# Moving the closing arithmetic of finished head groups behind the next step's products on VectorE, in a one-core decode attention kernel

## The chip, the core and the metric

The kernel runs on one core of a Trainium2 chip. The metric is device time in microseconds (us) of one execution, from first to last instruction of the core with what lies around it. Smaller is better. Several engines of the core run side by side, each with a queue of its own that it works off in order: TensorE (PE in the profile, PEld its weight loads), VectorE (DVE), ScalarE (ACT), GpSimd (POOL) and SyncE (SP), which here issues nearly all DMA transfers. An engine that reaches an instruction whose input isn't there waits, and everything behind it in its queue waits with it.

## The reference, cut to what matters

One decode step (one new token, batch of 2) of a pre-norm transformer block: attention with 32 heads of 128 over a cache of 8192 positions, and a gated feed-forward part. All tensors are bf16.

```python
def _A_ref(x, k_cache, v_cache, wq, wo):          # x: [2, 1, 512], caches: [2, 32, 8192, 128]
    q = (x @ wq).reshape(B, Sq, Hq, Dh).transpose(0, 2, 1, 3)
    scores = jnp.einsum("bhqd,bhkd->bhqk", q, k_cache) * (Dh ** -0.5)
    p = _softmax(scores, axis=-1)
    o = jnp.einsum("bhqk,bhkd->bhqd", p, v_cache)
    return o.transpose(0, 2, 1, 3).reshape(B, Sq, Hq * Dh) @ wo

h  = x + _A_ref(_layernorm(x), A_k_cache, A_v_cache, A_wq, A_wo)
h2 = h + _B_ref(_layernorm(h), B_W_gate, B_W_up, B_W_down)   # ((relu(x Wg) * (x Wu)) Wd)
```

Nearly all of the data are the two caches: 2 x 2 x 32 x 8192 x 128 values of two bytes, 268 MB, each read once.

## The kernel before, in words

**Steps.** The cache is worked through in steps. Steps 0 to 14 take four heads of one batch row each (a "quad"; `Q = LASTQ = 14`), and two last half steps, `p0` and `p1`, take two heads each. A quad's K tile and V tile are 8.39 MB each, [128 partitions x 32768] bf16. Three such buffers exist (`bufs`). Step i has its K in buffer 2i mod 3 and its V in buffer 2i+1 mod 3, so V of step i+1 goes where K of step i was, and K of step i+2 where V of step i was.

**What a step does.** `scores_pe(s)` (L329 on) lets TensorE and ScalarE compute the scores of the last 24 to 32 of the tile's 256 slots of 128 values. `products(s)` (L374 to L378) lets VectorE multiply the remaining slots by the query, one instruction of up to 128 x 29696 values, and `scores(s)` (L388 to L402) adds the products up in four halvings (L396), a reduction (L398) and a maximum (L402). `largest_of_own(s)` (L411 to L420) finds the maximum per head and issues the exponentials on ScalarE, `place_own(s)` (L422 to L426) spreads them into the operand `pg`, and `values(s, u0, u1)` (L443 to L454) issues products u0 to u1 of 64 that multiply the exponentials with V on TensorE.

**Groups.** After steps 3, 7 and 11 four quads are complete, after step 14 three more. `diagonals(i)` (L456) then gathers the group's unnormalised output in PSUM (`o_ps`). What closes a group is the function `close(i)` (L318 to L322), four parts: `own_sums(i)` (L297 to L302, VectorE, prepares the sums of exponentials in `zc`), `sums(i)` (L304 to L308, a TensorE product with ones that gives the denominators in `z_ps`), `shares(i)` (L310 to L312, VectorE, the reciprocal `rz`) and `normalise(i)` (L314 to L316, VectorE, output times reciprocal into `ocol`). In the loop (L518 to L556) `close(i - 1)` stands in steps 4, 8 and 12, behind the step's first eight value products.

**W_o's first rows.** In step 12 the kernel also calls `spread(0, b)` (L479 to L488, two VectorE products that lay 16 finished heads out in `qrep`), and, after eight more value products, `lay_rows(0, ..., scalar=True)` (L490 to L497): two TensorE products into `or_ps` and one ScalarE copy into `orow`.

**What sets the order.** The schedule is written by hand (`manual_schedule`): each engine executes its instructions in the order of the program text. SyncE issues a load when its buffer is free: V of step i+1 behind `scores(i)`, K of step i+2 behind `values(i)`. All of these loads go through one queue, and the transfers follow each other in it, each split over the 16 DMA engines.

**The end.** After the loop come the last quad, `p0` and `p1`, the loads of W_o (`wo`), the gate, up and down weights (`wgu`, `wd_sb`), the output product, the second normalisation and the feed-forward part (L651 to L723). The last weights to arrive are those of `wd_sb`, needed by the products `d_ps` of L712.

Of the kernel before, what the change touches and what calls it, by code (L numbers as in the profile page):

```python
# [13 lines left out]
def _free(t, offset, dims):  # L14

    return bass.AP(tensor=t.tensor, offset=t.offset + offset, ap=[t.ap[0]] + [list(d) for d in dims])
# [7 lines left out]
def kernel(  # L24
# [15 lines left out]
    B, Sq, D = A_x.shape  # L40
# [117 lines left out]
    Q = LASTQ  # L158

    def load_tile(cache, s, dst, pieces=1):  # L160
        h = NH * s.g + (0 if s.quad else 2 * s.k)
        n = s.nt * Dh
        w = n // pieces
        for k in range(pieces):
            nc.sync.dma_start(
                out=dst[:, k * w:(k + 1) * w], in_=_dram(cache, (s.b * Hkv + h) * Sk * Dh + k * w, [[n, P], [1, w]]),
            )
# [19 lines left out]
    with tc.manual_schedule():  # L187
# [94 lines left out]
        def place_q(s):  # L282
            nc.scalar.activation(out=qz[:, QZ - NH:QZ], in_=qTs[:, s.b, NH * s.g:NH * (s.g + 1)], func=ACT.Copy)

        groups = {3: (0, 0, 4), 7: (0, 4, 4), 11: (1, 0, 4), 14: (1, 4, 3)}
# [4 lines left out]
        def heads(i):  # L290
            if i > Q:
                k = i - Q - 1
                return B - 1, Hq - NH + 2 * k, 2, zc[:, B - 1, NQ - 1, 2 * k:2 * k + 2]
            b, g0, n = groups[i]
            return b, NH * g0, NH * n + (2 if i == Q else 0), zc[:, b, g0:g0 + n, :]

        def own_sums(i):  # L297
            b, g0, n = groups[i]
            nc.vector.tensor_tensor(
                out=zc[:, b, g0:g0 + n, :], in0=_free(zs, b * NQ + g0, [[1, n], [0, NH]]),  # L300
                in1=_free(own, 0, [[0, n], [1, NH]]), op=ALU.mult,
            )  # L302

        def sums(i):  # L304

            _, _, n, z = heads(i)
            z_ps[i] = ps.tile([P, n], f32, tag="mx", name="z_ps")
            nc.tensor.matmul(out=z_ps[i], lhsT=ones, rhs=z, start=True, stop=True)  # L308

        def shares(i):  # L310
            rzs[i] = small.tile([P, heads(i)[2]], f32, tag="rz", name="rz", bufs=2)
            nc.vector.reciprocal(out=rzs[i], in_=z_ps[i])  # L312

        def normalise(i):  # L314
            b, h0, n, _ = heads(i)
            nc.vector.tensor_tensor(out=ocol[:, h0:h0 + n, b], in0=o_ps[i][:, 0:n], in1=rzs[i], op=ALU.mult)  # L316

        def close(i):  # L318
            own_sums(i)
            sums(i)  # L320
            shares(i)
            normalise(i)  # L322

        scols = {
            i: qrep[:, c0:c0 + n].rearrange("p i d -> p (i d)").bitcast(f32)
            for i, c0, n in ((Q, 6, 4), (Q + 1, 10, 2), (Q + 2, 12, 2))
# [47 lines left out]
        def products(s, t0=0, t1=None):  # L374

            n = (s.nv if t1 is None else t1) - t0
            kv = _free(s.kt, t0 * Dh, [[Dh, n], [1, Dh]])
            nc.vector.tensor_tensor(out=kv, in0=kv, in1=_free(s.qr, 0, [[0, n], [1, Dh]]), op=ALU.mult)  # L378
# [9 lines left out]
        def scores(s):  # L388

            scol = scols[s.i]  # L390
            width = Dh
            while width > 8:
                half = width // 2
                lo = _free(s.kt, s.na * Dh, [[Dh, s.nv - s.na], [1, half]])
                hi = _free(s.kt, s.na * Dh + half, [[Dh, s.nv - s.na], [1, half]])
                nc.vector.tensor_tensor(out=lo, in0=lo, in1=hi, op=ALU.add)  # L396
                width = half
            nc.vector.tensor_reduce(  # L398
                out=scol[:, s.na:s.nv], in_=_free(s.kt, s.na * Dh, [[Dh, s.nv - s.na], [1, 8]]), axis=AXIS.X, op=ALU.add,
            )  # L400
            pms[s.i] = small.tile([P, 1], f32, tag="pm", name="pm", bufs=2)
            nc.vector.tensor_reduce(out=pms[s.i], in_=scol, axis=AXIS.X, op=ALU.max)  # L402
# [8 lines left out]
        def largest_of_own(s):  # L411
            pm32 = small.tile([P, 32], f32, tag="pm32", name="pm32")
            nc.vector.transpose(out=pm32, in_=_free(pms[s.i], 0, [[0, 32]]))  # L413
            hmax = small.tile([P, 1], f32, tag="hmax", name="hmax")
            nc.vector.tensor_reduce(out=hmax, in_=pm32, axis=AXIS.X, op=ALU.max)  # L415
            nmax = small.tile([P, 1], f32, tag="nmax", name="nmax", bufs=2)
            nc.vector.tensor_scalar_mul(nmax, hmax, -SCALE)  # L417
            nc.scalar.activation(  # L418
                out=ecol, in_=scols[s.i], func=ACT.Exp, scale=SCALE, bias=nmax, accum_out=zs[:, s.b, s.g:s.g + 1],
            )  # L420

        def place_own(s):  # L422
            nc.vector.tensor_tensor(  # L423
                out=s.pg, in0=_free(ecol, 0, [[VG, s.nt // VG], [0, NH], [1, VG]]),
                in1=_free(ownb, 0, [[0, s.nt // VG], [VG, NH], [1, VG]]), op=ALU.mult,
            )  # L426
# [16 lines left out]
        def values(s, u0, u1):  # L443

            r = slice(32 * (s.g % 4), 32 * (s.g % 4) + s.nh * VG)
            if u0 == 0:
                pv_ps[s.i] = ps2.tile([P, VG * Dh], f32, tag="o", name="pv_ps")
            for u in range(u0, u1):
                nc.tensor.matmul(  # L449
                    out=pv_ps[s.i][r, :], lhsT=s.pg[:, u].rearrange("p j t -> p (j t)"),  # L450
                    rhs=s.vt[:, u * VG * Dh:(u + 1) * VG * Dh], start=(u == 0), stop=(u == s.nt // VG - 1),
                )
            if u1 == s.nt // VG:
                nc.scalar.activation(out=pv[r, :], in_=pv_ps[s.i][r, :], func=ACT.Copy)  # L454
# [24 lines left out]
        def spread(k, b):  # L479

            h0, n, _ = SETS[k]
            nq = Dh // n
            sp = qrep[:, B * k + b, :]
            nc.vector.tensor_tensor(
                out=_free(sp, 0, [[nq, n], [1, nq]]), in0=_free(ocol, h0 * B + b, [[B, n], [0, nq]]),
                in1=_free(quot[n], 0, [[0, n], [1, nq]]), op=ALU.mult,
            )
            return sp  # L488

        def lay_rows(k, sps, scalar=False):  # L490

            r = SROWS[k]
            or_ps = ps.tile([P, B, r], f32, tag="mx")
            for b in range(B):
                nc.tensor.matmul(out=or_ps[:, b, :], lhsT=sps[b], rhs=rest[r], start=True, stop=True)
            if scalar:
                nc.scalar.activation(out=orow[k], in_=or_ps.rearrange("p b c -> p c b"), func=ACT.Copy)  # L497
            else:
                nc.vector.tensor_copy(orow[k], or_ps.rearrange("p b c -> p c b"))
# [18 lines left out]
        for i in range(Q):  # L518
            s = steps[i]
            scols[i] = small.tile([P, s.nt], f32, tag="scol", name="scol")  # L520
            scores_pe(s)
            place_q(steps[i + 1])
            products(s)
            scores(s)
            if i == Q - 2:
                load_tile(A_k_cache, steps[Q], steps[Q].kt)
            else:
                load_tile(A_v_cache, steps[i + 1], steps[i + 1].vt)
            if i == Q - 1:
                scores_pe(steps[Q])  # L530
            largest_of_own(s)
            if i == Q - 1:
                products(steps[Q], 0, NEXT)
            place_own(s)
            half = s.nt // VG // 2
            ahead = 8 if i - 1 in groups else 0
            if ahead:
                values(s, 0, ahead)
                close(i - 1)
            if i == 12:  # L540
                sps = [spread(0, b) for b in range(B)]
                values(s, ahead, 2 * ahead)
                ahead *= 2
                lay_rows(0, sps, scalar=True)
            values(s, ahead, half)
            if i == Q - 1:
                load_tile(A_k_cache, steps[Q + 1], steps[Q + 1].kt)
            values(s, half, 2 * half)
            if i in groups:
                diagonals(i)  # L550
            if i + 2 < Q:
                load_tile(A_k_cache, steps[i + 2], steps[i + 2].kt)
            elif i == Q - 2:
                load_tile(A_v_cache, steps[Q - 1], steps[Q - 1].vt)
            else:
                load_tile(A_k_cache, steps[Q + 2], steps[Q + 2].kt)  # L556


        s, p0, p1 = steps[Q:]
# [76 lines left out]
        sps = [[spread(k, b) for b in range(B)] for k in range(1, len(SETS))]  # L636
# [117 lines left out]
```

## Time and profile before

| what | value |
|---|---|
| median of three runs | 661.1 us (660.15 to 661.72) |
| the profiled execution: time | 660.24 us |
| its span in the trace | 658.5 us (so 1.74 us lie around the span) |
| VectorE busy | 557.5 us, 85% of the span |
| TensorE busy | 349.5 us, 53% |
| ScalarE busy | 123.1 us, 19% |
| queue of the loads | 281.09 MB, 99.0% of 16 engines' span, 427 GB/s |
| VectorE waiting for K tiles (L378) | 36.9 us in 11 waits |
| VectorE waiting for `z_ps` ahead of the reciprocal (L312) | 12.6 us in 4 waits, the longest 4.1 us |

All times below are us from the start of the span unless marked ns. A row of the timeline names start, duration, engine, line, operation, output and inputs, and in square brackets how long the engine had been idle just before and what ended the idle time. A row of the DMA view gives the time from issue to the landing of the last byte. The chain of waits is the work that ended last, followed back from the last instruction, at each step to what released it.

### The profile page before, as it was taken

What the parts mean: (1) busy time and instruction counts of PE and PEld (TensorE: products, weight loads), DVE (VectorE), ACT (ScalarE), POOL (GpSimd) and SP (SyncE); (2) the same over time, 40 slices, a digit from 0 to 9 for tenths busy, and PEclk for the clock granted to TensorE, in tenths of its full rate; (3) what the DMA queues carried; (4) which work ended last, traced back from release to release, by engine and by line L of the source; (5) the groups of instructions that cost most, each with busy time, mean ns of one, the idle gap of its engine ahead of it and who ended that gap; (6) DMA issues with size and microseconds to landing.
All of it is one profiled execution on the core that took longest, in us unless ns stands there. A gap on an engine that the chain in (4) does not pass through costs nothing.

```text
span 658.5 us, 5118 instructions
## 1 busy us (share of the span) xinstructions
PE 349.5 (53%) x2123; PEld 159.0 (24%) x2123; DVE 557.5 (85%) x248; ACT 123.1 (19%) x335; POOL 7.0 (1%) x35
## 2 busy tenths in 40 slices
PE   2530924709175380926538092562909458191997
PEld 1220311304022130312214031221403224030456
DVE  2399697988979799897979979896997969999981
ACT  1130030300203030030302103030210304201870
POOL 3000000000000000000000000000000000000000
PEclk9875876958678595877959587695958869686895
DMA  9999999999999999999999999999999999999997
GB/s 382 446 443 446 402 431 438 446 446 396 442 438 439 434 427 430 438 430 435 438 426 443 426 438 431 430 439 442 422 430 431 438 443 426 430 429 425 424 417 278
DMA packets 7946, 281.40 MB, mean 427 GB/s; under 512 B 882, under 2 KB 1780, under 8 KB 2804
## 3 DMA queue, kind: packets, MB, share of 16 engines
q1 hardware_dynamic: 7920, 281.09, 99.0%
q8 instruction: 16, 0.26, 0.1%
q14 instruction: 6, 0.05, 0.0%
q10 hardware_dynamic: 4, 0.00, 0.0%
HBM read 281.09 MB, written 0.00 MB: 427 GB/s over the span
## 4 chain that ended last, share of the span: by engine, by line
DVE 52%; DMA 29%; PE 18%; issue 1%; ACT 1%; SPq 0%; DVEq 0%; ACTq 0%
DMA tile<-in_A_k_cache_dram 29%; DVE tile L378 23%; DVE tile L396 22%; PE pv_ps L449 15%; DVE scol L398 3%; DVE pgq L423 1%; ACT ecol L418 1%; DVE pm L402 1%; DVE qrep L398 1%; PE o_ps L472 1%; DVE pm L413 0%; PE z_ps L308 0%; PE att_ps L505 0%; PE d_ps L701 0%; DVE hmax L415 0%
## 5 line engine op out<-in xcount | busy, mean ns | idle before, releaser
L449 PE MATMUL pv_ps<-tile,pgq 128*16 128x512 bf16 x960 | 240.7, 416 | 240.8 <-DVE pgq L423 227.8
L378 DVE TENSOR_TENSOR tile<-tile,qrep 128x29696 bf16<-128x29696 bf16 (+3 forms) x16 | 232.4, 14522 | 36.9 <-DMA tile<-in_A_k_cache_dram 36.9
L396 DVE TENSOR_TENSOR tile<-tile 128x14848 bf16<-128x14848 bf16 (+7 forms) x68 | 236.5, 3477 | 2.3
L449 PEld LDWEIGHTS <-pgq 128*16 128x16 bf16 x960 | 90.6, 96 | 379.9 <-DVE pgq L423 239.7
L353 ACT ACTIVATE tile<-t_ps 128x1024 bf16<-128x1024 bf16 x53 | 52.6, 1022 | 16.6 <-PE t_ps L352 16.1
L454 ACT ACTIVATE pv<-pv_ps 16x512 f32<-16x512 f32 (+1 forms) x16 | 9.4, 590 | 232.5 <-PE pv_ps L449 232.5
L418 ACT ACTIVATE ecol<-scol,nmax 128x256 bf16<-128x256 f32 x14 | 7.1, 508 | 201.0 <-DVE nmax L417 201.0
L352 PE MATMUL t_ps<-ident,tile 128*128 128x128 bf16 x424 | 31.7, 226 | 16.5 <-DMA tile<-in_A_k_cache_dram 16.5
L343 PE MATMUL row_ps<-tile,qz 128*24 128x512 bf16 (+1 forms) x98 | 29.6, 383 | 18.9 <-ACT tile L353 18.9
L352 PEld LDWEIGHTS <-tile 128*128 128x128 bf16 x424 | 25.4, 102 | 31.4 <-DMA tile<-in_A_k_cache_dram 17.1
L398 DVE TENSOR_REDUCE scol<-tile 128x232 f32<-128x1856 bf16 (+1 forms) x14 | 28.9, 2068 | 0.5
L423 DVE TENSOR_TENSOR pgq<-ecol,ownb 128x1024 bf16<-128x1024 bf16 x15 | 10.4, 692 | 10.3 <-ACT ecol L418 10.3
L384 ACT ACTIVATE tile<-tile 128x128 bf16<-128x128 bf16 x60 | 17.6, 294 | 1.9 <-DVE tile L378 1.9
L378 DVE TENSOR_TENSOR tile<-tile,qpair 128x4096 bf16<-128x4096 bf16 (+3 forms) x4 | 15.5, 3884 | 0.0
L252 DVE CAST tile<-q_ps 2x512 bf16<-2x512 f32 x8 | 5.4, 679 | 10.9 <-PE q_ps L249 10.9
L343 PEld LDWEIGHTS <-qz 128*24 128x24 bf16 (+1 forms) x98 | 7.8, 92 | 28.3 <-issue 22.8
L249 PE MATMUL q_ps<-tile,xn 128*2 128x512 bf16 x32 | 10.2, 486 | 8.4 <-DMA tile<-in_A_wq_dram 8.4
L370 ACT ACTIVATE scol<-sc_ps 32x24 f32<-32x24 f32 (+1 forms) x56 | 11.7, 210 | 7.7 <-PE sc_ps L365 7.2
L365 PE MATMUL sc_ps<-ident_f,tile 24*128 24x24 f32 (+2 forms) x68 | 7.2, 221 | 11.0 <-ACT tile L361 11.0
L361 ACT ACTIVATE tile<-row_ps 24x512 f32<-24x512 f32 (+2 forms) x17 | 10.0, 586 | 13.5 <-PE row_ps L343 13.5
L312 DVE RECIPROCAL rz<-z_ps 128x16 f32<-128x16 f32 (+1 forms) x4 | 0.9, 236 | 12.6 <-PE z_ps L308 12.6
L384 ACT ACTIVATION_READ_ACCUMULATOR tile<-tile 128x1 f32 x60 | 11.2, 187 | 0.0
(130 smaller groups left out, 130.8 us busy)
## 6 DMA issues: line engine op xcount, KB each, us to landing
tile<-in_A_k_cache_dram SPq DMA_DIRECT2D x2, 4096.0 KB, 21.7
tile<-in_A_wq_dram SPq DMA_DIRECT2D x1, 4096.0 KB, 12.4
tile<-in_A_v_cache_dram SPq DMA_DIRECT2D x1, 4096.0 KB, 19.4
tile<-in_A_v_cache_dram SPq DMA_DIRECT2D x4, 1024.0 KB, 20.5
tile<-in_A_wo_dram SPq DMA_DIRECT2D x1, 2048.0 KB, 23.8
tile<-in_B_W_gate_dram SPq DMA_DIRECT2D x2, 688.0 KB, 13.6
tile<-in_B_W_up_dram SPq DMA_DIRECT2D x2, 688.0 KB, 12.4
tile<-in_A_wo_dram SPq DMA_DIRECT2D x1, 1024.0 KB
```

Of the source, the lines that this page charges most:

```text
L249: nc.tensor.matmul(out=q_ps, lhsT=xn[:, c, :], rhs=wq_sb[:, c, n0:n0 + 4 * Dh], start=(c == 0), stop=(c == KC - 1),)
L343: nc.tensor.matmul(out=row_ps, lhsT=z, rhs=s.kt[:, (nv + c0 + k) * Dh:(nv + c0 + k + 4) * Dh], start=(u == 0), stop=(u == U - 1),)
L352: nc.tensor.transpose(t_ps[:, k, :], s.kt[:, t * Dh:(t + 1) * Dh], ident)
L353: nc.scalar.activation(out=s.kt[:, (nv + c0) * Dh:(nv + c0 + TPC) * Dh], in_=t_ps.rearrange("p t s -> p (t s)"), func=ACT.Copy,)
L370: nc.scalar.activation(out=scols[s.i][r, nv:s.nt].rearrange("p (u t) -> p t u", t=4), in_=sc_ps[r, :, :, j], func=ACT.Copy,)
L378: nc.vector.tensor_tensor(out=kv, in0=kv, in1=_free(s.qr, 0, [[0, n], [1, Dh]]), op=ALU.mult)
L384: nc.scalar.activation(out=kv, in_=kv, func=ACT.Copy, accum_out=scols[s.i][:, t:t + 1])
L396: nc.vector.tensor_tensor(out=lo, in0=lo, in1=hi, op=ALU.add)
L398: nc.vector.tensor_reduce(out=scol[:, s.na:s.nv], in_=_free(s.kt, s.na * Dh, [[Dh, s.nv - s.na], [1, 8]]), axis=AXIS.X, op=ALU.add,)
L418: nc.scalar.activation(out=ecol, in_=scols[s.i], func=ACT.Exp, scale=SCALE, bias=nmax, accum_out=zs[:, s.b, s.g:s.g + 1],)
L423: nc.vector.tensor_tensor(out=s.pg, in0=_free(ecol, 0, [[VG, s.nt // VG], [0, NH], [1, VG]]), in1=_free(ownb, 0, [[0, s.nt // VG], [VG, NH ...
L449: nc.tensor.matmul(out=pv_ps[s.i][r, :], lhsT=s.pg[:, u].rearrange("p j t -> p (j t)"), rhs=s.vt[:, u * VG * Dh:(u + 1) * VG * Dh], start= ...
```

## The change

`close` is taken apart. `own_sums(i - 1)` now stands ahead of the step's first eight value products, `sums(i - 1)` still behind them, and `shares` and `normalise` of the group are issued one step later, in steps 5, 9 and 13, directly behind `products(s)` and ahead of `scores(s)`. The two `spread` products and `lay_rows(0)` move from step 12 to the same place in step 13 (`Q - 1`), behind `normalise(11)`. No instruction is added or dropped, and no load is moved in the program text.

```diff
-        def close(i):
-            own_sums(i)
-            sums(i)
-            shares(i)
-            normalise(i)
-
...
             scores_pe(s)
             place_q(steps[i + 1])
             products(s)
+            if i - 2 in groups:
+                shares(i - 2)
+                normalise(i - 2)
+            if i == Q - 1:
+                lay_rows(0, [spread(0, b) for b in range(B)], scalar=True)
             scores(s)
...
             ahead = 8 if i - 1 in groups else 0
             if ahead:
+                own_sums(i - 1)
                 values(s, 0, ahead)
-                close(i - 1)
-            if i == 12:
-                sps = [spread(0, b) for b in range(B)]
-                values(s, ahead, 2 * ahead)
-                ahead *= 2
-                lay_rows(0, sps, scalar=True)
+                sums(i - 1)
             values(s, ahead, half)
```

## The prediction

> **What bounds the kernel now.** I read the page first. VectorE is busy most, but the load queue is never idle at all:
>
> ```profile
> PE 349.5 (53%) x2123; PEld 159.0 (24%) x2123; DVE 557.5 (85%) x248; ACT 123.1 (19%) x335; POOL 7.0 (1%) x35
> q1 hardware_dynamic: 7920, 281.09, 99.0%
> ```
>
> So the question is where VectorE's idle time matters. The waits by engine give VectorE 36.9 us in 11 waits for K tiles (L378) and 12.6 us in 4 waits for `z_ps` (L312). Three of those four are what the change removes; the timeline of VectorE shows them and what stands behind them. Steps 4 and 5, and the start of step 6:
>
> ```profile
> 228.01 0.26 DVE L312 RECIPROCAL rz<-z_ps 128x16 f32<-128x16 f32 x1 [3.71 <-PE z_ps L308]
> 228.31 0.18 DVE L316 TENSOR_TENSOR ocol<-o_ps,rz 128x16 bf16<-128x16 f32 x1
> 228.40 15.62 DVE L378 TENSOR_TENSOR tile<-tile,qrep 128x29696 bf16<-128x29696 bf16 x1
> ...
> 265.88 15.63 DVE L378 TENSOR_TENSOR tile<-tile,qrep 128x29696 bf16<-128x29696 bf16 x1 [1.87 <-DMA tile<-in_A_k_cache_dram]
> ```
>
> After the stall of 3.71 us step 5 starts at once, late; yet step 6 waits 1.87 us for its K tile. The delay of step 5 was eaten by the next wait. Step 8 is the same: 4.13 us of stall, step 9's products at 383.37 instead of some 1.6 us earlier, then 1.48 us of waiting for K in step 10 (at 420.45). Starts of products that waited for K lie 38.6 to 38.7 us apart (72.72, 111.28, 150.01, 188.61; 265.88, 304.56, 343.16). A step's K and V are 2 x 8.39 MB, so the stream runs at 16.78 MB / 38.63 us = 434 GB/s, and the table by stretches has 433 to 435 GB/s and a DMA share of 1.00 in nearly all of them. Through step 12 the kernel is bound by the stream.
>
> Step 12 is different, and the place that can matter. Behind its stall there is no wait for K:
>
> ```profile
> 499.21 15.09 DVE L378 TENSOR_TENSOR tile<-tile,qrep 128x28672 bf16<-128x28672 bf16 x1 [4.08 <-DMA tile<-in_A_k_cache_dram]
> ...
> 533.63 0.17 DVE L299 TENSOR_TENSOR zc<-zs,own 128x16 f32<-128x16 f32 x1
> 537.93 0.26 DVE L312 RECIPROCAL rz<-z_ps 128x16 f32<-128x16 f32 x1 [4.13 <-PE z_ps L308]
> 538.23 0.18 DVE L316 TENSOR_TENSOR ocol<-o_ps,rz 128x16 bf16<-128x16 f32 x1
> 538.32 0.48 DVE L484 TENSOR_TENSOR qrep<-ocol,quot 128x128 bf16<-128x128 bf16 x2
> 538.72 15.08 DVE L378 TENSOR_TENSOR tile<-tile,qrep 128x28672 bf16<-128x28672 bf16 x1
> ```
>
> From here the chain of waits runs over VectorE alone, with gaps only for the exponentials (0.73 us each), up to 637.4, and then through the short tail of TensorE and VectorE to the end. VectorE's own work sets the end from 538 on, the stream before.
>
> Now the landings. The DMA view and SyncE's timeline give step 13's K tile:
>
> ```profile
> 511.74 0.33 SPq L165 DMA_DIRECT2D tile<-in_A_k_cache_dram  x1
> ```
> ```profile
> tile<-in_A_k_cache_dram SPq DMA_DIRECT2D x1, 26.0
> ```
>
> It was issued at 511.74 and landed 26.0 us later, at 537.74. A second reading agrees: the K tile of step 12 came at 499.21, and TensorE waited for the V tile of step 13 until 576.47, four transfers later; 77.26 / 4 = 19.315 us each, which puts K of step 13, the second of the four, at 537.84. I take 537.8, with 0.1 of doubt. So VectorE's stall of 4.13 us in step 12 covers a wait for K that would have lasted nearly as long: from 533.8 to 537.8.
>
> **The change part by part.** The sum is made on the profiled execution (time 660.24, span 658.5).
>
> *Steps 4 and 8, stalls removed.* 3.71 + 4.13 = 7.84 us of idle time go. What is late next is K: for step 5 issued at 201.69, 25.6 us to landing, so 227.3; for step 9 issued at 355.77, 26.0 us, so 381.8. Step 5's products move from 228.40 to 227.3 (1.1 us earlier), step 9's from 383.37 to 381.8 (1.6). Both steps end the same way: waiting for K of steps 6 and 10, whose landing this doesn't move. Worth 0.
>
> *Steps 5 and 9, work added.* Reciprocal and product behind `products`: 228.01 to about 228.47, some 0.46 us each. Cover: step 6 and step 10 wait 1.87 and 1.48 us for K as it is, and get 1.1 and 1.6 us more by the earlier start. Cost 0; without that cover it would be 0.9 us in all.
>
> *Loads that follow.* V of steps 6 and 10 is issued behind `scores` of steps 5 and 9. Their issue (261.55 and 416.52) moves some 0.6 and 1.1 us earlier. K of the same step is still landing then (265.88, 420.45), so the transfer stands in the queue anyway: 0. All other issues keep their place; no queue is passed.
>
> *Step 12, the stall.* Step 13's products start when K is there, 537.8, not at 538.72: -0.9 us.
>
> *Step 13, the moved work.* From the start of the reciprocal to the start of the products, 537.93 to 538.72 by the timeline, 538.80 by the chain: 0.87 us for reciprocal (0.27 and 0.03 to the next), product (0.18) and two spreads (0.40). Behind `products` they stand between 552.9 and 553.8, on the path, with nothing idle around: +0.87 us. The inputs are long there, so they wait for nothing. The durations are those of the same instructions; between a dispatch that overlaps (0.79) and the chain's 0.87 I take the latter.
>
> *TensorE and ScalarE.* `lay_rows(0)` moves from 539.68 to behind step 13's `scores_pe`, which ended at 557.1; its spreads are ready at 553.8, so TensorE waits for nothing, 3.3 us to spare. What stands behind it on TensorE and ScalarE is the last quad's `scores_pe`, done at 564.3 and first needed when VectorE reduces over the scores at 605: 0.2 us of copy and two short products are lost in 40 us. In step 12, 0.2 us of TensorE go. `own_sums` already ran at once (533.63) and `sums` keeps its place behind eight value products; 0.
>
> *The end.* Even a gain could pass only in part. The last piece of `wd_sb` was issued at 649.51 and landed 5.7 us later, at 655.2:
>
> ```profile
> 654.25 1.32 PE L712 MATMUL d_ps<-hm,tile 128*128 128x2 bf16 x44 [0.26 <-DVE hm L708]
> ```
>
> Its four products are the last of these 44 (to 655.57), so they run some 0.25 us after the landing. VectorE's path could become about 0.25 us shorter before the stream sets the end again.
>
> Sum: 0 + 0 + 0 - 0.92 + 0.87 + 0 = -0.05, say -0.1 with the doubt of K's landing: 660.2 against the profiled 660.24. The median lies 0.9 above the profiled execution; against it 661.1 - 0.1 = **661.0**.
>
> **Two rules of the skill.** The Trainium skill's page "Perfetto Trace Analysis" (Identifying the Most-Contended Engine, and Optimization Strategy) says that the engine with the highest occupancy is to be improved first, by finding the gaps between its slices and starting what they wait for sooner. By occupancy that is VectorE, and this change does just that; it is the second rival below. The page "DMA: Bandwidth & Descriptors" (Specifications) gives 435 GB/s as the ceiling of the fabric into SBUF. The 434 GB/s above agrees, and speaks against that rival; the same table's limit of about 358 GB/s for HBM per core is exceeded here by this trace.
>
> **The rivals.**
>
> *The late V loads had cost the stream something.* K of step 11 came 40.16 us after K of step 10 (420.45 to 460.61), the only such interval after step 1; 38.6 would be usual: 1.56 us lost, in the step whose V load (416.52) was issued latest, 3.9 us ahead of K's landing. If the late issue is the cause, the change gives that back: all that follows moves, 661.1 - 1.56 = 659.5. Against: V of step 6 was issued 4.3 us ahead, nearly as late, and K of step 7 came on time (38.68); and in 440 to 461 the queue of instruction packets (q8) had a packet of its own on the same engines, which would come in any order of the work. Chance 0.10.
>
> *VectorE's idle time comes through.* All three stalls, 3.71 + 4.13 + 4.13 = 11.97 us, less nothing: 649.1. It needs a stream of 281 MB that ends 12 us sooner, at 435 GB/s already. Chance 0.02; a tenth of it is no likelier.
>
> *K of step 13 lands late (slower).* In step 12 the four instructions now stand in the shadow of that landing, in step 13 in none. If K comes at 538.72 or later, nothing is gained at the stall and 0.87 is paid: 662.0. It decides from a landing 0.05 us later than I read: each us later costs one, up to 0.87. For: one transfer in the trace was late by 1.56 (above). Against: the other intervals agree within 0.1. Chance 0.14; it is over 0.2% only together with some scatter of the medians.
>
> *Nothing of it is seen, because the reciprocal waits as before.* `sums` ends some 15 us before `shares` in the new order, so this can't be; no chance.
>
> **How the numbers follow.** Forecast 0.74, with its own range 660.4 to 661.6 (doubt of the landing and scatter of medians); early stream 0.10; idle time through 0.02; late K 0.14. The range goes from 659.4 (early stream) to 662.3 (late K, with 0.3 of scatter). 0.2% is 1.3 us, about what a measurement of this kernel can tell from no change. Faster by more: 0.02 + 0.09 of the 0.10, so 0.11. Slower by more: 0.05 of the late K and 0.05 for scatter, so 0.10. Within: 0.79.
>
> **What would show it.** Right: no wait ahead of L312 in steps 4, 8, 12; waits for K ahead of L378 in all steps 1 to 13, some 4 us where the stalls were (36.9 becomes about 48 in 14 waits); products of step 13 at 537.8, its halvings again at about 553.8; the end unchanged. Wrong: K of step 13 landing elsewhere than 38.6 us behind step 12's, K of step 11 on time, or a gap on VectorE behind 553.8 that isn't in the profile of before.

## The result and the profile after

The changed kernel takes 659.88 us (median of 16 executions, 659.32 to 660.42), the kernel before 661.01 us beside it (16 executions, 659.77 to 662.18). The ratio is 0.9984, with a 95% interval of 0.9977 to 0.9991: 1.1 us faster, more than the 0.1 us that I worked out, and less than 0.2%. The form of the two lists says more than the medians. Before, six executions lie near 660.1 and ten above 660.7; after, none lies above 660.42. The profiled execution of before (660.24) was one of the short ones; that of after took 660.0, with a span of 658.2.

The page of the changed kernel, first and third part, and VectorE's waits for K (us in total, times, longest):

```profile
PE 356.3 (54%) x2123; PEld 161.3 (25%) x2123; DVE 557.2 (85%) x248; ACT 123.0 (19%) x335; POOL 7.1 (1%) x35
q1 hardware_dynamic: 7920, 281.09, 99.0%
```
```profile
DVE tile L372 <- DMA tile<-in_A_k_cache_dram: 49.0, 14, 5.5
```

The wait ahead of the reciprocal is gone in steps 4, 8 and 12, and the wait for K has grown from 36.9 us to 49.0 us, in 14 steps instead of 11. VectorE's timeline around steps 5 and 6 (L372 is L378 of before):

```profile
227.42 15.63 DVE L372 TENSOR_TENSOR tile<-tile,qrep 128x29696 bf16<-128x29696 bf16 x1 [3.04 <-DMA tile<-in_A_k_cache_dram]
242.97 0.25 DVE L312 RECIPROCAL rz<-z_ps 128x16 f32<-128x16 f32 x1
243.25 0.18 DVE L316 TENSOR_TENSOR ocol<-o_ps,rz 128x16 bf16<-128x16 f32 x1
...
266.01 15.63 DVE L372 TENSOR_TENSOR tile<-tile,qrep 128x29696 bf16<-128x29696 bf16 x1 [2.73 <-DMA tile<-in_A_k_cache_dram]
```

Step 5 starts as soon as its K is there, and step 6 waits 2.73 us for its own: the 3.71 us of stall became two longer waits for the stream. Steps 12 and 13:

```profile
533.41 0.17 DVE L299 TENSOR_TENSOR zc<-zs,own 128x16 f32<-128x16 f32 x1
537.55 15.09 DVE L372 TENSOR_TENSOR tile<-tile,qrep 128x28672 bf16<-128x28672 bf16 x1 [3.97 <-DMA tile<-in_A_k_cache_dram]
552.56 0.25 DVE L312 RECIPROCAL rz<-z_ps 128x16 f32<-128x16 f32 x1
552.84 0.18 DVE L316 TENSOR_TENSOR ocol<-o_ps,rz 128x16 bf16<-128x16 f32 x1
552.93 0.48 DVE L478 TENSOR_TENSOR qrep<-ocol,quot 128x128 bf16<-128x128 bf16 x2
553.34 7.62 DVE L390 TENSOR_TENSOR tile<-tile 128x14336 bf16<-128x14336 bf16 x1
```

The halvings of step 13 begin at 553.34 instead of 553.84; 0.22 us of this were there already when K of step 12 came (498.99 instead of 499.21). At the end, VectorE's last cast waits longer for TensorE, which waits for `wd_sb`:

```profile
655.38 0.17 DVE L712 CAST y<-d_ps 128x8 bf16<-128x8 f32 x1 [1.68 <-PE d_ps L707]
```

Before, this cast began at 655.60 after 1.41 us. The end moved by 0.2 us because the last piece of `wd_sb` landed that much earlier (at 655.03 instead of 655.26); the cast begins 0.35 us behind that landing in both. So nothing of the 0.5 us on VectorE's path came through, it went into waiting for the stream. Between these two executions there is little to explain: 0.24 us. The 1.1 us between the medians are long executions that the changed kernel doesn't have.

### The profile page after: what moved, and what is told of

Its sections match the earlier page's. It is cut to its first block, busy times and chain, and to the rows that moved or that the text cites. A ratio compares the mean times of both kernels' runs of the same rounds, so it can differ in the third digit from the quotient of the medians.

```text
span 658.2 us, 5118 instructions
## 1 busy us (share of the span) xinstructions
PE 356.3 (54%) x2123; PEld 161.3 (25%) x2123; DVE 557.2 (85%) x248; ACT 123.0 (19%) x335; POOL 7.1 (1%) x35
## 4 chain that ended last, share of the span: by engine, by line
DVE 47%; DMA 32%; PE 19%; ACT 1%; issue 1%; DVEq 0%; ACTq 0%
DMA tile<-in_A_k_cache_dram 30%; DVE tile L372 21%; DVE tile L390 20%; PE pv_ps L443 15%; DVE scol L392 2%; DMA tile<-in_A_wq_dram 2%; PE q_ps L249 1%; DVE pgq L417 1%; DVE pm L396 1%; ACT ecol L412 1%; DVE qrep L392 1%; PE o_ps L466 1%; PE att_ps L499 0%; PE d_ps L696 0%; DVE pm L407 0%
## 5 line engine op out<-in xcount | busy, mean ns | idle before, releaser
L443 PE MATMUL pv_ps<-tile,pgq 128*16 128x512 bf16 x960 | 245.0, 422 | 233.5 <-DVE pgq L417 220.7
L372 DVE TENSOR_TENSOR tile<-tile,qrep 128x29696 bf16<-128x29696 bf16 (+3 forms) x16 | 232.4, 14524 | 49.0 <-DMA tile<-in_A_k_cache_dram 49.0
L346 PE MATMUL t_ps<-ident,tile 128*128 128x128 bf16 x424 | 33.1, 232 | 17.9 <-DMA tile<-in_A_k_cache_dram 17.9
L378 ACT ACTIVATE tile<-tile 128x128 bf16<-128x128 bf16 x60 | 17.6, 296 | 1.9 <-DVE tile L372 1.9
L372 DVE TENSOR_TENSOR tile<-tile,qpair 128x4096 bf16<-128x4096 bf16 (+3 forms) x4 | 15.5, 3882 | 0.0
L378 ACT ACTIVATION_READ_ACCUMULATOR tile<-tile 128x1 f32 x60 | 11.3, 188 | 0.0
L359 PEld LDWEIGHTS sc_ps<-ident_f,tile 24*128 24x128 f32 (+2 forms) x68 | 5.5, 137 | 19.4 <-ACT tile L355 19.4
## 6 DMA issues: line engine op xcount, KB each, us to landing
tile<-in_A_v_cache_dram SPq DMA_DIRECT2D x4, 1024.0 KB, 21.1
```

The lines of the kernel that those rows point to most:

```text
L346: nc.tensor.transpose(t_ps[:, k, :], s.kt[:, t * Dh:(t + 1) * Dh], ident)
L359: nc.tensor.transpose(sc_ps[:, t].rearrange("p u j -> p (u j)"), rows[:, t * P:(t + 1) * P], ident_f[0:nh * U, 0:nh * U],)
L378: nc.scalar.activation(out=kv, in_=kv, func=ACT.Copy, accum_out=scols[s.i][:, t:t + 1])
L443: nc.tensor.matmul(out=pv_ps[s.i][r, :], lhsT=s.pg[:, u].rearrange("p j t -> p (j t)"), rhs=s.vt[:, u * VG * Dh:(u + 1) * VG * Dh], start= ...
```

## The experiments

Four theories were to be told apart. A: the gain lies on VectorE's path from step 12 on. B: the stalls of steps 4 and 8 made the V loads of steps 6 and 10 late, and in some executions that costs the stream time. C: long executions come from TensorE's clock in the last stretch. D, as the rival of B later: it is the place of the group's arithmetic that counts, not the time of the loads.

**The kernel before, twice more.** No edit.

> The kernel before once more, for the spread of its own executions: 16 of them lay between 659.8 and 662.2, six near 660.1 and ten from 660.7 up, while 16 of the changed kernel lay between 659.3 and 660.4. Theory A (path of VectorE): from the landing of K of step 12 to step 13's halvings pass 54.6 us in each execution, and a long execution differs where K of step 13 landed against the end of the stall. Theory C (TensorE's clock in the last stretch): that part is the same in a long execution, and the extra 1 to 2 us lie behind 605, where the clock rises later than 5.0 us after the last quad's value products begin, so that VectorE waits longer for TensorE ahead of the last maximum (0.58 us in the trace shown).

> The same kernel before a second time, for another trace of it; A and C expect of it what they expect of the first. If both traces are of short executions (near 660.1), neither is told apart by these two.

Medians 660.70 (12 executions, 659.64 to 662.53) and 660.61 (11, 659.58 to 662.81), 10 of the 23 above 660.7. The second trace is of a longer execution, span 659.4. Its SyncE issued V of step 6 at about the same time as in the trace shown first (261.61, there 261.55), but behind that load its stream is slow. SyncE's timeline, then the table by stretches (start:end, length, busy times of PE, PEld, DVE, ACT and POOL, PEclk, DMA share, GB/s):

```profile
261.61 0.33 SPq L165 DMA_DIRECT2D tile<-in_A_v_cache_dram  x1
```
```profile
262.00:269.00 7.00, 4.88 (x12) 1.61 (x13) 4.80 (x5) 0.60 (x2) 0.00 (x0) 0.50 0.94 365
```

The execution of before that the prediction used has 431 GB/s in that stretch:

```profile
262.00:269.00 7.00, 4.94 (x14) 1.67 (x15) 4.33 (x5) 0.60 (x2) 0.00 (x0) 0.55 1.00 431
```

Such a stretch of 7 us can differ by some 20 GB/s with where its packets begin and end (the changed kernel has 412 there). The trace's single packets show it without that doubt: a packet of 64 KB takes 2.42 us on its engine, and in the long execution the first packets of this V load took 0.7 us more on average over all 16 engines; 0.03 us in the short one. K of step 7 then came 39.4 us after K of step 6, where 38.6 to 38.7 are usual:

```profile
265.44 15.62 DVE L378 TENSOR_TENSOR tile<-tile,qrep 128x29696 bf16<-128x29696 bf16 x1 [1.37 <-DMA tile<-in_A_k_cache_dram]
...
304.83 15.62 DVE L378 TENSOR_TENSOR tile<-tile,qrep 128x29696 bf16<-128x29696 bf16 x1 [3.77 <-DMA tile<-in_A_k_cache_dram]
```

What this cost at the end can't be read off as simply. On VectorE's path it is gone by step 12: K of step 12 came at 499.25 (499.21 in the short execution), the end of step 12's stall is 38.72 us behind it in both, and step 13's halvings begin at 553.88 (553.84). A wait for K is a wait for the last of 16 engines, and the last one falls behind in jumps of 1 to 2 us, in the short execution between V of step 10 and K of step 11, in the long one at V of step 9. Middle engines carry the loss on: by the landing records the middle engine is 0.9 us later than in the short execution when the last weights begin to arrive (653.4 against 652.4 for the fourth piece of `wd_sb`). The last piece then landed at 656.26 instead of 655.26: the last engine's landings of two pieces that usually lie 0.3 us apart were 1.9 us apart here (653.86 and 655.79). The end waits for it:

```profile
656.61 0.17 DVE L717 CAST y<-d_ps 128x8 bf16<-128x8 f32 x1 [2.05 <-PE d_ps L712]
```

The cast begins 0.35 us behind that landing, as in the short execution. So the extra 1.0 us is the stream's, which speaks against A; how much of it is the slow start and how much the engine that fell behind at the end, one trace doesn't tell. C had the place right (behind 605) and the cause wrong: the clock rose at 611.3, not later than in the short execution (613.0), and the maximum of L431 came at 638.34 (638.31).

**The two halves of the change.** `only_4_8` moves the arithmetic of groups 3 and 7 alone, `only_12` that of group 11 and W_o's first rows alone:

```diff
 # only_4_8, against the changed kernel
-            if i - 2 in groups:
+            if i - 2 in (3, 7):
...
-            if i == Q - 1:
-                lay_rows(0, [spread(0, b) for b in range(B)], scalar=True)
...
+            if i == 12:
+                values(s, 0, ahead)
+                close(i - 1)
+                sps = [spread(0, b) for b in range(B)]
+                values(s, ahead, 2 * ahead)
+                ahead *= 2
+                lay_rows(0, sps, scalar=True)
 # only_12, against the changed kernel
-            if i - 2 in groups:
+            if i - 2 == 11:
...
+            elif ahead:
+                values(s, 0, ahead)
+                close(i - 1)
```

> The change in steps 4, 5, 8 and 9 alone; step 12 closes its group and lays W_o's first rows out as before. Theory A (all from VectorE's path behind step 12): as the kernel before, a ratio of 1.000 to it, executions spread from 659.8 to 662.2. Theory B (the late V loads of steps 6 and 10 had cost the stream time): as the changed kernel, 659.9, ratio 0.998, and K of step 11 comes 38.6 us after K of step 10.

> The change in steps 12 and 13 alone; groups 3 and 7 close as before with stalls of 3.7 and 4.1 us. Theory A: as the changed kernel, 659.9, ratio 0.998, executions within 659.3 to 660.4. Theory B: as the kernel before, ratio 1.000, with 659.8 to 662.2.

| kernel | median, us | executions | above 660.7 | ratio to before, 95% |
|---|---|---|---|---|
| `only_4_8` | 659.87 | 659.57 to 660.59 | 0 of 11 | 0.9989 (0.9981 to 0.9998) |
| `only_12` | 660.61 | 659.73 to 662.24 | 6 of 12 | 1.0000 (0.9990 to 1.0010) |

The effect is in steps 4, 5, 8 and 9, as far as the intervals tell. The half that I had called the place that can matter is worth nothing, as its sum of -0.92 and +0.87 said. A falls. One detail of B falls too: in `only_4_8` K of step 11 still comes 39.5 us after K of step 10 (420.27 to 459.77), and in the changed kernel 39.6. That late landing doesn't depend on when the V loads are issued.

**Less and more stall.** In the kernel before, groups 3 and 7 close behind 4 or 16 value products instead of 8:

```diff
-            ahead = 8 if i - 1 in groups else 0
+            ahead = (8 if i == 12 else 4) if i - 1 in groups else 0     # close_at_4; 16 in close_at_16
```

> The kernel before, with groups 3 and 7 closed behind four value products instead of eight; step 12 as before. The stalls in steps 4 and 8 fall from 3.7 and 4.1 us to about 2, so that steps 5 and 9 start on their K tiles and V of steps 6 and 10 is issued about 1.1 us earlier, as in the changed kernel. Theory B (issue of these V loads too late by a hair): as the changed kernel, 659.9, ratio 0.998 to 0.999, executions within 659.3 to 660.6. Theory D (the place of the group's arithmetic behind the products does it, not the time of the loads): as the kernel before, ratio 1.000, executions up to 662.

> The kernel before, with groups 3 and 7 closed behind sixteen value products; step 12 as before. The stalls grow to about 6 to 7 us and V of steps 6 and 10 is issued 2 to 3 us later, at about 264 and 419, where K of the same step lands between 264 and 266 and between 419 and 420.5 on its 16 engines. Theory B: in every execution the stream loses 1 to 3 us at each of the two places, 662.5 to 666, ratio 1.002 to 1.008. A stream that doesn't mind (my forecast's step): as the kernel before, since step 6 and step 10 still find some wait for K: ratio 1.000.

`close_at_4`: 659.93 (659.50 to 660.35, none of 11 above 660.7), ratio 0.9985 (0.9976 to 0.9994). `close_at_16`: 663.82 (663.23 to 664.45), ratio 1.0050 (1.0038 to 1.0063). The place of the arithmetic is that of before in both, so D falls. In `close_at_16` V of steps 6 and 10 is issued at 263.71 and 420.43, and both places lose in the trace:

```profile
262.00:269.00 7.00, 2.79 (x7) 0.93 (x8) 6.07 (x7) 0.60 (x2) 0.00 (x0) 0.50 0.86 337
417.00:424.00 7.00, 1.06 (x3) 0.38 (x4) 6.00 (x9) 0.60 (x2) 0.00 (x0) 0.50 0.79 300
```

By the landing records the middle one of the 16 engines needed 21.0 and 21.1 us from K to V at these two places, where 19.3 is usual: 1.7 + 1.8 = 3.5 us, of the 3.9 us by which the median exceeds that of the changed kernel. And its chain of waits ends on the stream, not on VectorE:

```profile
649.18 8.56 DMA tile<-in_B_W_down_dram
657.75 0.05 issue
657.79 0.49 PE d_ps L712 x8
```

**The changed kernel made late again.** Steps 5 and 9 get 2, 4 or 7 reductions on VectorE whose results nothing uses (added work, 0.33 to 0.37 us each), ahead of `scores`:

```diff
+            if i in (5, 9):
+                junk = small.tile([P, 4], f32, tag="junk", name="junk")     # 2, 4 or 7
+                for k in range(4):
+                    nc.vector.tensor_reduce(out=junk[:, k:k + 1], in_=ecol, axis=AXIS.X, op=ALU.max)
```

> The changed kernel with two VectorE reductions of 256 elements, whose results nothing uses, in steps 5 and 9 behind the group's arithmetic: some 0.9 us, which brings the issue of V of steps 6 and 10 back to where it was before (some 2.4 us ahead of the first engine that is done with K), with no stall and with TensorE's order as after. Theory B: executions spread as before, 659.7 to 662.3, median 660.5 to 661.2. Theory D: as the changed kernel, 659.9, none above 660.6.

> The changed kernel with four VectorE reductions whose results nothing uses in steps 5 and 9 (0.33 to 0.37 us each by the trace with two of them). V of steps 6 and 10 is issued some 1.8 us ahead of the first engine that is done with K, as in the kernel before. Theory B: the spread of before, executions from 659.7 to above 661.5, median 660.4 to 661.2. Theory D: as the changed kernel, 659.9, none above 660.6.

> The same with seven reductions: V of steps 6 and 10 is issued some 0.6 to 0.9 us ahead of the first engine. Theory B: each of the two places loses 0.5 to 1.2 us in every execution, between after and the close behind sixteen (663.8): 661.0 to 662.5. Theory D: as the changed kernel, 659.9; VectorE still waits for K in steps 6 and 10.

Medians 660.00 (659.72 to 660.80; 2 of 11 above 660.7), 660.61 (659.87 to 662.31; 5 of 11) and 662.51 (661.73 to 662.98; 6 of 6), the last with a ratio of 1.0031 (1.0020 to 1.0042). With two reductions the median hardly moved, where B expected 660.5 to 661.2; they were shorter than planned, and the loads less late than before. Four gave back the spread of before, with no stall and TensorE's order as after. This table sets all of it in order by the time from the issue of V until the first of the 16 engines ends its last packet of K, read from the packets of one trace of each kernel:

| kernel | V of step 6, us ahead | V of step 10, us ahead | median, us | above 660.7 |
|---|---|---|---|---|
| `close_at_4` | 3.4 | 3.4 | 659.93 | 0 of 11 |
| `only_4_8` | 3.0 | 2.9 | 659.87 | 0 of 11 |
| after | 2.7 | 2.7 | 659.88 | 0 of 16 |
| `after_late` | 2.5 | 2.4 | 660.00 | 2 of 11 |
| before (trace shown first) | 2.0 | 1.8 | 661.01 | 10 of 16 |
| `only_12` | 2.0 | 1.6 | 660.61 | 6 of 12 |
| `after_late4` | 1.7 | 1.5 | 660.61 | 5 of 11 |
| `after_late7` | 0.6 | 0.0 | 662.51 | 6 of 6 |
| `close_at_16` | -0.1 | -0.3 | 663.82 | 5 of 5 |

In the kernels with 2.7 us or more no execution is long, in those with 2.0 down to 1.5 about half are, in those with 0.6 or less all are. In the trace of before all other 8.39 MB loads behind step 1 are issued 2.8 us ahead or more, but for V of step 14 with 2.3 (measured against the load before it in the queue). `close_at_4` has 2.3 us there too and no long execution, so where between 2.0 and 2.7 us the loss begins isn't settled. The lead isn't the same in each execution of a kernel: the two further traces of before have 2.3 and 2.1 us (`b_again1`, a short execution) and 1.7 and 2.1 (`b_again2`, the long one, slow at the load with 1.7). So a row stands for its kernel only within some 0.3 us.

**More work in the queue.** If lateness matters because the queue runs short, a piece of V issued early should cover for it. In steps 5 and 9 the last 24 of 256 slots of V go by a transfer of their own as soon as TensorE's scores are done with that part of K: once in the kernel before with its stalls, once with the seven reductions.

```diff
+            if i in (5, 9):
+                load_cols(A_v_cache, steps[i + 1], steps[i + 1].vt, s.nv * Dh, TILE)
             products(s)
...
+            elif i in (5, 9):
+                load_cols(A_v_cache, steps[i + 1], steps[i + 1].vt, 0, s.nv * Dh)
             else:
                 load_tile(A_v_cache, steps[i + 1], steps[i + 1].vt)
```

> The kernel before with all its stalls, but in steps 5 and 9 the last 24 of V's 256 slots per partition (0.79 MB, 1.8 us of stream) are loaded by a transfer of their own, issued as soon as the scores that TensorE computes are done with that part of K, some 13 us ahead of the rest. So 1.8 us more of work stands in the queue when the rest of V is issued late. Theory B: as the changed kernel, 659.9, ratio 0.998 to 0.999, none above 660.6. Theory D: as the kernel before, ratio 1.000, executions up to 662.

> The same seven reductions, and in steps 5 and 9 the last 24 of V's 256 slots per partition as a transfer of their own, issued as soon as TensorE's scores are done: 1.8 us more of work in the queue when the rest is issued late. Theory B: the loss goes, 659.9 to 660.5, with VectorE's timeline as in the run without the piece. If the loss comes from VectorE's path (its own lateness in steps 5 and 9): 661.0 to 662.5 as without the piece.

`before_early_piece`: 660.26 (659.89 to 660.74, 1 of 11 above 660.7), ratio 0.9994 (0.9985 to 1.0003). With V of steps 6 and 10 issued as late as before (2.1 and 1.8 us ahead of the end of K) and all stalls in place, the long executions are nearly gone. The median is still 0.4 us above the changed kernel's, and the interval of the ratio reaches 1. `after_late7_piece`: 660.93 (659.88 to 663.43), 1.6 us less than without the piece (662.51), but 7 of 12 above 660.7. In its trace VectorE is about as late at step 6 (it waits 0.63 us for K, 0.45 without the piece), but the rest of V of steps 6 and 10 was issued 1.0 and 0.7 us ahead of the end of K, against 0.6 and 0.0 without the piece; so not all of the difference is the piece's. The first of the two kernels is the cleaner test, and it says that the loss was the queue's and not VectorE's; both medians miss what B expected. The executions of `after_late7_piece` up to 663.43, longer than any without the piece, are not explained: its one trace is of the shortest execution, and 1.8 us of piece with 0.7 to 1.0 us of lead make 2.5 to 2.8, where the table has few or no long ones.

**The piece in all steps.** The same on the changed kernel in steps 0 to 11, as a try at a version that beats both:

> The changed kernel with V's last slots (24 or 32 of 256) as a transfer of their own, issued early, in all steps 0 to 11, so that no V load is near to late. Theory B: at these places nothing is left to gain, since the changed kernel issues its V loads 2.7 us or more ahead: 659.6 to 660.2, the same as the changed kernel within 0.05%. A gain of 0.5 us or more would mean that small losses are left at other steps.

660.62 (660.18 to 661.03), none as short as the changed kernel's median: 0.7 us slower than it, against 0.05% expected. The twelve more transfers cost time on balance, where and why isn't shown; nothing was gained at the loads that the changed kernel issues 2.7 us ahead or more. The changed kernel stays the fastest version but for `only_4_8` and `close_at_4`, which equal it.

## Why the prediction was right and wrong

- *What bounds the kernel.* Right: the stream through step 12. The 11.97 us of VectorE's idle time that were removed went into longer waits for K: I had expected about 48 us in 14 waits and the trace has 49.0 in 14. The 1.1 us came another way (below). The Trainium skill's "Perfetto Trace Analysis" (Identifying the Most-Contended Engine) was told only in part in the prediction: by occupancy VectorE comes first, but for DMA the page takes HBM utilisation in place of occupancy. The loads, at 427 GB/s against the 435 that the prediction cites, then come first, and that agrees with these runs.
- *Steps 4, 5, 8 and 9: stalls and work.* Right on VectorE: the stalls became waits for K, the added 0.4 us of work is covered.
- *Loads that follow.* This is the step that failed. I put the earlier issue of V at 0, because "K of the same step is still landing then (265.88, 420.45), so the transfer stands in the queue anyway". I measured the distance to the last of 16 engines, 4 us. The distance to the first was 2.0 and 1.8 us, and with about that much half of the executions are long. In the one that a trace caught, the start of the V load is slow, by 0.7 us over all engines; the profiled execution was one of those that lose nothing, so the trace that I read didn't show the cost. The step that I priced at 0 is worth 1.1 us in the median, and as far as the two halves tell it is the whole change.
- *Steps 12 and 13.* Right: products at 537.55 (537.8 predicted), halvings at 553.34 (553.8), the four instructions 0.78 us instead of 0.87, and `only_12` at a ratio of 1.0000.
- *The end.* Right in kind, but the 0.25 us that VectorE's path was to have before the stream sets the end weren't there: in the trace of before the last four products begin at 655.32, 0.05 us behind the landing at 655.26. None of the 0.5 us came through. In four of the six traces from the kernel before, the changed kernel and its two halves (before, after, `b_again2`, `only_4_8`; not `b_again1` and `only_12`) the cast begins 0.35 us behind the last landing of `wd_sb`, so the stream sets the end there.
- *The rivals.* The first one, which I gave 0.10, named the mechanism that acted. Its evidence was wrong both ways: K of step 11 comes 39.2 to 40.5 us after K of step 10 in every kernel's trace, with the V loads early or late (only in `b_again2` it is 38.6, as the last engine had fallen behind at V of step 9 already). And the V load of step 6 that I held against it had come through unharmed by luck: in `b_again2` the same load lost. Its price, 1.56 us, was taken from that unrelated delay; the measured difference is 1.1 us. The late K that was to make it slower wasn't seen.
- *The number.* 661.0 was forecast as the likeliest, and 659.88 came, outside the 660.4 to 661.6 of the forecast's own account and within the range only because this rival had set its lower end at 659.4. That the range held is luck for the account that I believed in. The change is faster by 0.16%, inside the 0.2% that I had called no difference, and still clear of 1 by its interval.

## What to carry to other kernels

In a kernel bound by its loads, idle time of a compute engine is worth nothing by itself, but it counts by what it does to the issue of the next load; measure that load's lead against the first DMA engine to run out of work, not against the landing that the compute engine waits for. A profile is one execution: where medians are compared, look at the list of executions first, since a cost that strikes in half of them can be absent from the trace that you read. And a small lead can be bought without the change at all: closing the groups behind four value products instead of eight gave the same time.

## What the runs showed of the hardware

Where the two V loads of 8.39 MB were issued 2.7 us or more ahead of the end of the first engine's last packet, none of 38 executions was above 660.7; where they were issued 1.5 to 2.0 us ahead, about half were. In the long execution that a trace caught, the load with 1.7 us of lead started slowly on all 16 engines, also on those that had 3.5 us of work left. Why the late ones are slow too, and why in some executions only, stays open; the traces show the packets, not what they waited for. The Trainium skill's "DMA: Bandwidth & Descriptors" (Specifications) gives a first-byte latency of about 0.6 us for loads from this queue; in `after_late7`, with that much of a lead at one place and none at the other, the loss against the changed kernel was 2.6 us. The 16 engines also don't run level: in the trace of before 0.7 us lie between the first and the last of them at K of step 0, 2.3 us one transfer later and 3.0 us at K of step 12, and every wait for K is a wait for the last.
